# Strassen slots of a fused attention and MoE kernel: product 3 between 6 and 7, the two runs of 512-column products joined behind 7, product 4 last

## The chip, the core and the metric

The kernel runs on one core of a Trainium2 chip. The metric is device time in microseconds (us); three runs of the kernel before gave 1327.15, 1327.16 and 1327.39, the median is 1327.16. Engines are named as the profile names them: PE (TensorE matmuls), PEld (TensorE weight loads), DVE (VectorE), ACT (ScalarE), POOL (GpSimd), SP (SyncE, which issues the DMAs).

## What is computed

Three layers follow each other: a retention attention (2 batches, 8 heads, 768 positions), a mixture of 8 experts whose gate is normalised by 8 rounds of row and column scaling, and a feed-forward block with a tanh.

```python
x = attn_out.transpose(0, 2, 1, 3).reshape(1536, 512)
P = sinkhorn(exp(x @ w_gate - max))            # 1536 x 8
out = 0
for e in range(8):
    h = maximum(x @ w1[e], 0)                  # 1536x512 @ 512x1024
    out += P[:, e:e+1] * (h @ w2[e])           # 1536x1024 @ 1024x512
h = out @ w_in                                 # 1536x512 @ 512x2048
return (h - tanh(h)) @ w_out
```

The change lies in the expert loop.

## The kernel before

Operands are split into a high and a low part (`w1h`, `w1l`, `hhi`, `hlo`, ...), so that every product of two tiles is three matmuls: high by high, high by low, low by high.

**Slots.** The expert layer is a loop over 96 slots (`for s in range(NS)`, L585): 16 half experts `u`, 3 blocks `b` of 512 tokens, and `p` in (0, 1). One slot computes two 128x512 tiles of `h` from a 2 by 2 block product in Strassen's form with seven products. `product(ps, s, i, start)` (L572) issues product `i`: six matmuls of 256 columns (L579, L581, L582, twice) into a half of a PSUM bank. A slot has two banks, `pa` (named `ha` in the trace) and `pb` (`hb`), from a pool of four.

**What ties the products together inside a slot.** Product 1 goes to `pa` low; ACT copies it to `s12` low (L600). Products 2 and 5 go to the two halves of `pb`; ACT copies product 5 to `s5` (L607). Product 6 is added to `pa` low; ACT copies the sum to `s12` high (L609). Product 3 is added to `pb` high, over product 5, so it may start only when the copy to `s5` has read it. Product 7 is added to `pa` low, so it may start only when the copy to `s12` high has read that half. DVE then forms `pa` high from `pa` low and `s5` (L617), product 4 is added to `pa` low, and DVE adds `s12` to all of `pb` (L628). `pa` and `pb` are then the two rows of `h` before the ReLU. `relu_hi` (ACT, L508) and `relu_lo` (DVE, L513) write the high and low part of the ReLU to `hhi` and `hlo`, which have two buffers each.

**Second products.** A finished row is put on the list `parts`; `second` (L468) issues its twelve matmuls of 512 columns against `w2h` and `w2l` (L477, L478, L480) into four banks `yp`. After the second row of a slot with `p = 1` the four banks hold a finished sum and `evac` (L483, DVE) adds them to `yacc`, one call for each bank.

**Order of a slot before.** The order is written out by hand, and each engine runs its instructions in it: products 1, 2, 5, 6; the second products of the slot before's row `a` (12 matmuls); the helpers of `fill[s]`; product 7; the second products of the slot before's row `b` (12 matmuls); two calls of `evac`; the helpers of `fillb[s]`; product 4; product 3; two calls of `evac`; the helpers of `fillc[s]`. The row `b` of a slot gets its ReLU only in the next slot (`pend`). Only slot 0, which has no row behind it, runs products 1, 2, 5, 6, 3, 7, 4.

**Helpers.** `fill`, `fillb` and `fillc` hold, for each slot, the work of other stages: loading, summing and splitting the next expert's weights (`w_load`, `w_sum`, `w1_split`, `w2_split`), conversion of the last layer's weights (`conv`), the gate (`gate1`, `gate2`, `stage`, some with a small matmul), and in the first slots the splitting of the remaining tokens (`blocks1`, `blocks2`).

Of the kernel before, what the change touches and what calls it, by code (L numbers as in the profile page):

```python
# [14 lines left out]
ALU = mybir.AluOpType  # L15
# [12 lines left out]
TPB = BT // 128  # L28
# [22 lines left out]
def kernel(  # L51
# [9 lines left out]
    nc = tc.nc  # L61
# [10 lines left out]
    def bank(name):  # L72
        return psh.tile([128, 512], F32, tag="h", name=name)
# [107 lines left out]
    for i in range(12):  # L181
# [9 lines left out]
        out=g[:, 129:257], data0=lamt.to_broadcast([H, 128]), data1=one8, initial=1.0,  # L191
# [7 lines left out]
        out=dtab,  # L199
# [4 lines left out]
    for hh in range(2):  # L204
        src = gscr[:, 129:257].rearrange("(n two) m -> two n m", two=2)[hh]
        nc.sync.dma_start(
            out=lq[64 * hh:64 * hh + 64],
# [257 lines left out]
    parts = []  # L465


    def second(ps, tiles=range(TPB), late=False):  # L468
        for u, b, q, i, a, c, first, last in ps:
            if first and 0 in tiles:  # L470
                ypsum[u, b] = [psy.tile([128, 512], F32, tag=f"y{n}", name=f"yp{u}_{b}_{n}") for n in range(TPB)]
            for terms in ((0, 1), (2,)) if late else ((0, 1, 2),):
                for t in tiles:
                    ts = slice(128 * t, 128 * t + 128)
                    yp = ypsum[u, b][t]
                    if 0 in terms:
                        nc.tensor.matmul(out=yp, lhsT=a[:, ts], rhs=w2h[q][:, i], start=first, stop=False)  # L477
                        nc.tensor.matmul(out=yp, lhsT=a[:, ts], rhs=w2l[q][:, i], start=False, stop=False)  # L478
                    if 2 in terms:
                        nc.tensor.matmul(out=yp, lhsT=c[:, ts], rhs=w2h[q][:, i], start=False, stop=last)  # L480
        return (u, b) if last else None

    def evac(u, b, t):  # L483
        yp = ypsum[u, b]
        if t == 0 and u in (0, NU):
            yacc[b] = yp_.tile([128, TPB, DM], F32, tag=f"y{b}", name=f"yacc{u}_{b}")
        y = yacc[b][:, t]
        if u == 0:
            nc.vector.tensor_copy(out=y, in_=yp[t])
        elif u == NU:  # L490
            nc.scalar.activation(out=y, in_=yp[t], func=ACTF.Copy)
        elif u == 1 or u > NU:
            nc.vector.tensor_tensor(out=y, in0=yp[t], in1=y, op=ALU.add)
        else:
            nc.vector.scalar_tensor_tensor(out=y, in0=yp[t], scalar=prob[:, b * TPB + t, u // 2:u // 2 + 1], in1=y,  # L495
                                           op0=ALU.mult, op1=ALU.add)
        if u == NU + NQ - 1:
            n0 = t % B * S + (b * TPB + t) // B * CH
            nc.sync.dma_start(out=out[n0:n0 + 128, :], in_=y)
# [6 lines left out]
    def relu_hi(ps, name):  # L506
        a = hp.tile([128, 512], F32R, tag="hhi", name=f"hhi{name}")
        nc.scalar.activation(out=a, in_=ps, func=ACTF.Relu)  # L508
        return a

    def relu_lo(ps, a, name):
        c = hp.tile([128, 512], F32R, tag="hlo", name=f"hlo{name}")
        nc.vector.scalar_tensor_tensor(out=c, in0=ps, scalar=0.0, in1=a.bitcast(F32), op0=ALU.max, op1=ALU.subtract)  # L513
        return c
# [13 lines left out]
    fill = {s: [] for s in range(LASTS + 4)}  # L528
    fillb = {s: [] for s in range(LASTS + 4)}
# [34 lines left out]
    for n in range(nconv):  # L564
        s = s0 + n * (s1_ - s0) // nconv
# [6 lines left out]
    def product(ps, s, i, start):  # L572
        u, b, p = s // 6, s // 2 % 3, s % 2
        q = 2 * u + p
        kind, xi = XI[i]
        xh, xl = (x1[b][kind, j][:, xi].rearrange("p (k m) -> p k m", k=2) for j in range(2))
        for k in range(2):
            ws = slice(WI[i] + 128 * k, WI[i] + 128 * k + 128)
            nc.tensor.matmul(out=ps, lhsT=w1h[q][:, ws], rhs=xh[:, k], start=start and k == 0, stop=False,  # L579
                             skip_group_check=True)  # L580
            nc.tensor.matmul(out=ps, lhsT=w1h[q][:, ws], rhs=xl[:, k], start=False, stop=False, skip_group_check=True)  # L581
            nc.tensor.matmul(out=ps, lhsT=w1l[q][:, ws], rhs=xh[:, k], start=False, stop=k == 1, skip_group_check=True)  # L582

    pend = None
    for s in range(NS):  # L585
        if s == 1:
            yp_, sm = (ctx.enter_context(tc.tile_pool(name=n, bufs=1, reuse_waits="tile")) for n in ("yp", "sm"))
        if s == 4:
            attn.close()
            wps.append(ctx.enter_context(tc.tile_pool(name="wpc", bufs=1, reuse_waits="tile")))  # L590
            attn = ctx.enter_context(ExitStack())
            cp = attn.enter_context(tc.tile_pool(name="cp", bufs=1, side="right", reuse_waits="tile"))
        u, b, p = s // 6, s // 2 % 3, s % 2
        q = 2 * u + p
        pa, pb = bank(f"ha{s}"), bank(f"hb{s}")
        s12 = sn_.tile([128, 512], F32, tag="s12", name=f"s12_{s}")
        s5 = sn_.tile([128, 256], F32, tag="s5", name=f"s5_{s}")
        lo, hi = slice(0, 256), slice(256, 512)
        product(pa[:, lo], s, 1, True)
        nc.scalar.activation(out=s12[:, lo], in_=pa[:, lo], func=ACTF.Copy)  # L600
        if pend:
            hb = relu_hi(pend[0], f"b{s - 1}")
            lb = relu_lo(pend[0], hb, f"b{s - 1}")
            parts.append(pend[1] + (hb, lb, False, (s - 1) % 2 == 1))
        product(pb[:, lo], s, 2, True)
        product(pb[:, hi], s, 5, True)
        nc.scalar.activation(out=s5, in_=pb[:, hi], func=ACTF.Copy)  # L607
        product(pa[:, lo], s, 6, False)
        nc.scalar.activation(out=s12[:, hi], in_=pa[:, lo], func=ACTF.Copy)  # L609
        if pend:  # L610
            second([parts.pop(0)])
        for f in fill[s]:
            f()
        if s == 0:
            product(pb[:, hi], s, 3, False)
        product(pa[:, lo], s, 7, False)
        nc.vector.tensor_tensor(out=pa[:, hi], in0=pa[:, lo], in1=s5, op=ALU.add)  # L617
        done = second([parts.pop(0)]) if pend else None
        if done:
            evac(*done, 0)  # L620
            evac(*done, 1)
        for f in fillb[s]:
            f()
        product(pa[:, lo], s, 4, False)
        ha = relu_hi(pa, f"a{s}")
        if s > 0:
            product(pb[:, hi], s, 3, False)
        nc.vector.tensor_tensor(out=pb, in0=pb, in1=s12, op=ALU.add)  # L628
        la = relu_lo(pa, ha, f"a{s}")
        parts.append((u, b, q, 1, ha, la, p == 0, False))  # L630
        pend = (pb, (u, b, q, 0))
        if done:
            evac(*done, 2)
            evac(*done, 3)
        for f in fillc[s]:
            f()
    hb = relu_hi(pend[0], "bz")
    parts.append(pend[1] + (hb, relu_lo(pend[0], hb, "bz"), False, True))


    attn.close()
# [5 lines left out]
    def sub(v):  # L647
        u, b, f = NU + v // 12, v // 4 % 3, v % 4
        return u, b, 2 * u + f // 2, f % 2, f
# [32 lines left out]
    for v in range(NV + 2):  # L682
        if v < NV:
            u, b, q, i, f = sub(v)
# [10 lines left out]
        for part_ in due:  # L695
            done = second([part_], late=v == NV + 1)
# [52 lines left out]
```

## Time and profile before

| | |
|---|---|
| median of three runs | 1327.16 us |
| span of the profiled execution, first to last instruction | 1325.3 us |
| around the span (median less span; no separate total time of the profiled execution is given) | 1.9 us |
| PE busy | 1313.7 us, 99% of the span |
| DVE, ACT, POOL busy | 69%, 40%, 21% |
| TensorE clock granted | 0.998 of full speed in the mean |

The profile is one execution. Times of a row are counted from the span's first instruction. In the timeline a matmul's printed duration overlaps its successor's, since matmuls are pipelined; the distance from one start to the next is what a matmul costs the stream.

### The profile page before, as it was taken

To read this page: it belongs to the slowest core of one execution; us is meant where nothing else is said; L and a number is where in the kernel's file an instruction comes from. 1 tells how busy PE (TensorE), PEld (TensorE's weight loads), DVE (VectorE), ACT (ScalarE), POOL (GpSimd) and SP (SyncE) were. 2 spreads that over 40 slices of the span, in tenths; PEclk is the share of its full clock that TensorE was granted. 3 is DMA by queue.
4 is the path that set the end of the run, shared out by engine and by line. 5 is a ranking of instruction groups with operands and counts; after the bars stand their busy time and mean duration, and the time that the engine had idled before them with its cause. 6 is when DMAs were issued, how large, how long until landed. Compare 5 with 4: busy or idle time off the path is not lost.

```text
span 1325.3 us, 20925 instructions
## 1 busy us (share of the span) xinstructions
PE 1313.7 (99%) x8383; PEld 1163.0 (88%) x8383; DVE 913.2 (69%) x1698; ACT 527.9 (40%) x1029; POOL 274.1 (21%) x323
## 2 busy tenths in 40 slices
PE   8999999999999999999999999999999999999998
PEld 6889999999999999999999999999999888888887
DVE  4886676757657575757666675757654487788887
ACT  1443332233323232323322332323232578776764
POOL 4611011212213131222212221322210102020200
PEclk9999999999999999999999999999999999999999
DMA  9501120212312122212222132221211100000001
GB/s 299 173 32 33 33 72 25 69 59 65 100 55 81 57 68 61 76 56 69 72 64 68 57 100 69 69 68 57 69 36 33 33 32 32 32 32 32 32 32 64
DMA packets 37138, 85.00 MB, mean 64 GB/s; under 512 B 4136, under 2 KB 13872, under 8 KB 37040
## 3 DMA queue, kind: packets, MB, share of 16 engines
q1 hardware_dynamic: 37040, 83.67, 19.7%
q8 instruction: 65, 1.06, 0.3%
q14 instruction: 33, 0.27, 0.1%
HBM read 72.11 MB, written 11.55 MB: 63 GB/s over the span
## 4 chain that ended last, share of the span: by engine, by line
PE 96%; DVE 2%; DMA 1%; issue 0%; SPq 0%; ACT 0%; DVEq 0%; ACTq 0%
PE yp L480 16%; PE yp L477 16%; PE yp L478 16%; PE ha L579 7%; PE ha L582 7%; PE ha L581 7%; PE hb L579 5%; PE hb L581 5%; PE hb L582 5%; PE g L691 3%; PE g L689 3%; PE g L690 3%; DMA qkv<-in_qkv 1%; PE tr L523 0%; PE o L277 0%
## 5 line engine op out<-in xcount | busy, mean ns | idle before, releaser
L508 ACT ACTIVATE hhia<-ha 128x512 fp32r<-128x512 f32 x96 | 57.5, 599 | 469.9 <-PE ha L582 467.6
L579 PE MATMUL ha<-xsh,w1h 128*128 128x256 f32 x576 | 162.4, 282 | 1.7 <-ACT s L600 1.7
L582 PE MATMUL ha<-xsh,w1l 128*128 128x256 f32 x576 | 161.2, 280 | 0.0
L581 PE MATMUL ha<-xsl,w1h 128*128 128x256 f32 x576 | 160.8, 279 | 0.0
L456 POOL TENSOR_TENSOR c<-c,d 128x256 f32<-128x256 f32 x64 | 47.8, 746 | 544.0 <-DVE d L455 544.0
L478 PE MATMUL yp<-w2l,hhia 128*128 128x512 f32 x384 | 149.5, 389 | 0.0
L480 PE MATMUL yp<-w2h,hloa 128*128 128x512 f32 x384 | 149.5, 389 | 0.0
L477 PE MATMUL yp<-w2h,hhia 128*128 128x512 f32 x384 | 149.4, 389 | 0.0
L480 PE MATMUL yp<-w2h,hlob 128*128 128x512 f32 x380 | 148.7, 391 | 0.0
L478 PE MATMUL yp<-w2l,hhib 128*128 128x512 f32 x380 | 148.0, 390 | 0.0
L477 PE MATMUL yp<-w2h,hhib 128*128 128x512 f32 x380 | 147.9, 389 | 0.0
L617 DVE TENSOR_TENSOR ha<-ha,s 128x256 f32<-128x256 f32 x96 | 41.4, 432 | 141.2 <-PE ha L582 140.7
L628 DVE TENSOR_TENSOR hb<-hb,s 128x512 f32<-128x512 f32 x96 | 67.0, 697 | 91.5 <-PE hb L582 91.5
L495 DVE SCALAR_TENSOR_TENSOR yacc<-yp,prob,yacc 128x512 f32<-128x512 f32 x168 | 118.8, 747 | 9.0 <-PE yp L480 9.0
L579 PEld LDWEIGHTS ha<-xsh,w1h 128*128 128x128 f32 x576 | 108.2, 188 | 9.2 <-ACT s L600 1.9
L581 PEld LDWEIGHTS ha<-xsl,w1h 128*128 128x128 f32 x576 | 108.3, 188 | 7.4
L582 PEld LDWEIGHTS ha<-xsh,w1l 128*128 128x128 f32 x576 | 108.9, 189 | 0.0
L579 PE MATMUL hb<-xph,w1h 128*128 128x256 f32 x384 | 106.8, 278 | 0.0
L581 PE MATMUL hb<-xpl,w1h 128*128 128x256 f32 x384 | 106.4, 277 | 0.0
L582 PE MATMUL hb<-xph,w1l 128*128 128x256 f32 x384 | 106.2, 277 | 0.0
L480 PEld LDWEIGHTS yp<-w2h,hloa 128*128 128x128 f32 x384 | 72.1, 188 | 15.0
L480 PEld LDWEIGHTS yp<-w2h,hlob 128*128 128x128 f32 x380 | 71.4, 188 | 14.9
(159 smaller groups left out, 3332.8 us busy)
## 6 DMA issues: line engine op xcount, KB each, us to landing
wraw<-in_w SPq DMA_DIRECT2D x64, 512.0 KB, 4.7
d<-in_wio SPq DMA_DIRECT2D x64, 256.0 KB, 2.8
qkv<-in_qkv SPq DMA_DIRECT2D x23, 512.0 KB, 7.2
wscr<-c SPq DMA_DIRECT2D x64, 128.0 KB, 1.8
wraw<-wscr SPq DMA_DIRECT2D x16, 512.0 KB, 4.4
out<-yacc SPq DMA_DIRECT2D x12, 256.0 KB, 2.1
qkv<-in_qkv SPq DMA_DIRECT2D x2, 256.0 KB, 3.2
dtab<-gscr SPq DMA_DIRECT2D x1, 512.0 KB, 6.4
```

The lines of the kernel that those rows point to most:

```text
L456: nc.gpsimd.tensor_tensor(out=c1.bitcast(F32), in0=c1.bitcast(F32), in1=lo.bitcast(F32), op=ALU.mult)
L477: nc.tensor.matmul(out=yp, lhsT=a[:, ts], rhs=w2h[q][:, i], start=first, stop=False)
L478: nc.tensor.matmul(out=yp, lhsT=a[:, ts], rhs=w2l[q][:, i], start=False, stop=False)
L480: nc.tensor.matmul(out=yp, lhsT=c[:, ts], rhs=w2h[q][:, i], start=False, stop=last)
L495: nc.vector.scalar_tensor_tensor(out=y, in0=yp[t], scalar=prob[:, b * TPB + t, u // 2:u // 2 + 1], in1=y, op0=ALU.mult, op1=ALU.add)
L508: nc.scalar.activation(out=a, in_=ps, func=ACTF.Relu)
L579: nc.tensor.matmul(out=ps, lhsT=w1h[q][:, ws], rhs=xh[:, k], start=start and k == 0, stop=False, skip_group_check=True)
L581: nc.tensor.matmul(out=ps, lhsT=w1h[q][:, ws], rhs=xl[:, k], start=False, stop=False, skip_group_check=True)
L582: nc.tensor.matmul(out=ps, lhsT=w1l[q][:, ws], rhs=xh[:, k], start=False, stop=k == 1, skip_group_check=True)
L617: nc.vector.tensor_tensor(out=pa[:, hi], in0=pa[:, lo], in1=s5, op=ALU.add)
L628: nc.vector.tensor_tensor(out=pb, in0=pb, in1=s12, op=ALU.add)
L689: nc.tensor.matmul(out=ph, lhsT=w1h[q][:, ws], rhs=x2[b][0][:, k], start=k == 0, stop=False)
```

## The change

Slots 1 to 95 get the order 1, 2, 5, 6, 3, 7, then both rows of second products as one run of 24 matmuls, row `b` first, then the helpers of `fill[s]` and `fillb[s]`, then the ReLU of this slot's own row `b`, the four calls of `evac` where a sum is finished, product 4, the ReLU of row `a`, and the helpers of `fillc[s]`. `pend` is gone: row `b` is put on the list in its own slot. The flags for the first and the last part of a sum change places, because row `b` now comes first. The DVE sum into `pb` comes right behind product 3.

```diff
-        if pend:
-            hb = relu_hi(pend[0], f"b{s - 1}")
-            lb = relu_lo(pend[0], hb, f"b{s - 1}")
-            parts.append(pend[1] + (hb, lb, False, (s - 1) % 2 == 1))
         product(pb[:, lo], s, 2, True)
         product(pb[:, hi], s, 5, True)
         nc.scalar.activation(out=s5, in_=pb[:, hi], func=ACTF.Copy)
         product(pa[:, lo], s, 6, False)
         nc.scalar.activation(out=s12[:, hi], in_=pa[:, lo], func=ACTF.Copy)
-        if pend:
-            second([parts.pop(0)])
-        for f in fill[s]:
-            f()
-        if s == 0:
-            product(pb[:, hi], s, 3, False)
+        product(pb[:, hi], s, 3, False)
+        nc.vector.tensor_tensor(out=pb, in0=pb, in1=s12, op=ALU.add)
         product(pa[:, lo], s, 7, False)
         nc.vector.tensor_tensor(out=pa[:, hi], in0=pa[:, lo], in1=s5, op=ALU.add)
-        done = second([parts.pop(0)]) if pend else None
+        done = None
+        while parts:
+            done = second([parts.pop(0)])
+        for f in fill[s] + fillb[s]:
+            f()
+        hb = relu_hi(pb, f"b{s}")
+        parts.append((u, b, q, 0, hb, relu_lo(pb, hb, f"b{s}"), p == 0, False))
         if done:
-            evac(*done, 0)
-            evac(*done, 1)
-        for f in fillb[s]:
-            f()
+            for t in range(TPB):
+                evac(*done, t)
         product(pa[:, lo], s, 4, False)
         ha = relu_hi(pa, f"a{s}")
-        if s > 0:
-            product(pb[:, hi], s, 3, False)
-        nc.vector.tensor_tensor(out=pb, in0=pb, in1=s12, op=ALU.add)
-        la = relu_lo(pa, ha, f"a{s}")
-        parts.append((u, b, q, 1, ha, la, p == 0, False))
-        pend = (pb, (u, b, q, 0))
-        if done:
-            evac(*done, 2)
-            evac(*done, 3)
+        parts.append((u, b, q, 1, ha, relu_lo(pa, ha, f"a{s}"), False, p == 1))
         for f in fillc[s]:
             f()
-    hb = relu_hi(pend[0], "bz")
-    parts.append(pend[1] + (hb, relu_lo(pend[0], hb, "bz"), False, True))
```

## Rows read from the trace of the kernel before

**Rows 1.** The page: span, PE's busy time, the chain's share by engine.

```profile
span 1325.3 us, 20925 instructions
...
PE 1313.7 (99%) x8383; PEld 1163.0 (88%) x8383; DVE 913.2 (69%) x1698; ACT 527.9 (40%) x1029; POOL 274.1 (21%) x323
...
PE 96%; DVE 2%; DMA 1%; issue 0%; SPq 0%; ACT 0%; DVEq 0%; ACTq 0%
```

**Rows 2.** Busy time by stretch: slots 0 to 3, and slots 20 to 59.

```profile
60.57:100.53 39.96, 38.23 (x280) 34.47 (x278) 30.18 (x57) 19.62 (x40) 4.58 (x6) 1.00 0.08 27
...
266.98:678.07 411.09, 411.09 (x2643) 373.45 (x2641) 277.12 (x546) 129.38 (x269) 93.63 (x122) 1.00 0.22 69
```

**Rows 3.** Timeline of PE, one slot's turn: start, duration, line, tile.

```profile
604.52 0.40 PE L480 MATMUL yp<-w2h,hlob 128*128 128x512 f32 x1
604.76 0.28 PE L579 MATMUL ha<-xsh,w1h 128*128 128x256 f32 x1
...
605.46 0.28 PE L579 MATMUL hb<-xph,w1h 128*128 128x256 f32 x1
...
606.15 0.28 PE L579 MATMUL ha<-xph,w1h 128*128 128x256 f32 x1
...
608.08 0.28 PE L582 MATMUL hb<-xsh,w1l 128*128 128x256 f32 x1
...
608.88 0.39 PE L477 MATMUL yp<-w2h,hhia 128*128 128x512 f32 x1
...
611.60 0.28 PE L579 MATMUL ha<-xsh,w1h 128*128 128x256 f32 x1
...
612.30 0.39 PE L477 MATMUL yp<-w2h,hhib 128*128 128x512 f32 x1
```

**Rows 4.** Timeline of ACT in that slot: the copy to s5.

```profile
608.39 0.38 ACT L607 ACTIVATE s<-hb 128x256 f32<-128x256 f32 x1 [0.33 <-PE hb L582]
```

**Rows 5.** Timeline of PE, PEld and ACT in slot 0, products 6, 3, 7.

```profile
62.67 0.28 PE L582 MATMUL hb<-xsh,w1l 128*128 128x256 f32 x1
...
62.99 0.39 ACT L607 ACTIVATE s<-hb 128x256 f32<-128x256 f32 x1 [1.03 <-PE hb L582]
...
63.38 0.28 PE L582 MATMUL ha<-xsh,w1l 128*128 128x256 f32 x1
63.43 0.19 PEld L579 LDWEIGHTS hb<-xph,w1h 128*128 128x128 f32 x1
63.50 0.32 PE L579 MATMUL hb<-xph,w1h 128*128 128x256 f32 x1
...
63.65 0.28 PE L581 MATMUL hb<-xpl,w1h 128*128 128x256 f32 x1
...
64.11 0.28 PE L582 MATMUL hb<-xph,w1l 128*128 128x256 f32 x1
64.13 0.19 PEld L579 LDWEIGHTS ha<-xsh,w1h 128*128 128x128 f32 x1
...
64.36 0.28 PE L581 MATMUL ha<-xsl,w1h 128*128 128x256 f32 x1
...
64.83 0.28 PE L582 MATMUL ha<-xsh,w1l 128*128 128x256 f32 x1
```

**Rows 6.** Timeline of PE: product 1 of slot 1, right behind product 4.

```profile
66.96 0.28 PE L581 MATMUL ha<-xpl,w1h 128*128 128x256 f32 x1
...
67.53 0.28 PE L579 MATMUL hb<-xph,w1h 128*128 128x256 f32 x1
```

**Rows 7.** Timeline of DVE and PE, slots 3 and 4: tokens' low part and its reader.

```profile
97.57 1.22 DVE L133 TENSOR_TENSOR xsl<-ts,xsh 128x1024 fp32r<-128x1024 f32 x1
...
102.00 0.28 PE L581 MATMUL hb<-xsl,w1h 128*128 128x256 f32 x1
```

**Rows 8.** The page's groups: two of DVE's, busy, mean ns, idle before.

```profile
L628 DVE TENSOR_TENSOR hb<-hb,s 128x512 f32<-128x512 f32 x96 | 67.0, 697 | 91.5 <-PE hb L582 91.5
L495 DVE SCALAR_TENSOR_TENSOR yacc<-yp,prob,yacc 128x512 f32<-128x512 f32 x168 | 118.8, 747 | 9.0 <-PE yp L480 9.0
```

More of the change, by code (lines that the diff above doesn't have):

```diff
@@ L582, in product @@
             nc.tensor.matmul(out=ps, lhsT=w1l[q][:, ws], rhs=xh[:, k], start=False, stop=k == 1, skip_group_check=True)
-    pend = None
+    lo, hi = slice(0, 256), slice(256, 512)
     for s in range(NS):
@@ L597 @@
         s5 = sn_.tile([128, 256], F32, tag="s5", name=f"s5_{s}")
-        lo, hi = slice(0, 256), slice(256, 512)
         product(pa[:, lo], s, 1, True)
         nc.scalar.activation(out=s12[:, lo], in_=pa[:, lo], func=ACTF.Copy)
-        if pend:
-            hb = relu_hi(pend[0], f"b{s - 1}")
-            lb = relu_lo(pend[0], hb, f"b{s - 1}")
-            parts.append(pend[1] + (hb, lb, False, (s - 1) % 2 == 1))
         product(pb[:, lo], s, 2, True)
```

## The prediction

> **What bounds the kernel now.** I read the page first, then the busy times by stretch, then the timeline of PE at single matmuls, and last the timeline of slot 0, which already runs the order that the other slots are to get. PE is busy 1313.7 of 1325.3 us, and the chain that ended last is 96% PE [rows 1]. From slot 20 to slot 60 (the window is cut at the first matmul of product 1 in both) PE is busy for all of the 411.09 us [rows 2]: no wait opens a gap there, and a slot costs 411.09 / 40 = 10.277 us. So the time can change in two ways only: the pace of the stream, or a new wait in it.
>
> The pace is not the same everywhere, and this is what the reader is to see in the timeline. From 606.15 to 608.88 products 1, 2, 5 and 6 run in 2.73 us for 24 matmuls, 0.1135 each or 0.68 a product; a run of 512-column products takes 2.72 for 12, 0.227 each. Product 7, between the two runs, takes 0.70 (611.60 to 612.30), product 4, behind the second run, also 0.70 (604.76 to 605.46), and product 3 after it 0.69; the last matmul before product 4 takes 0.24 instead of 0.227 [rows 3]. So 256-column matmuls have a fast pace, 0.1133, and a slow one, about 0.1177, which they fall into behind a run of 512-column products. In these slots the slow pace ends as product 4 ends. Six slow matmuls cost 6 x 0.0044 = 0.026. The excess of a slot over the fast pace, 10.277 - 42 x 0.1133 - 24 x 0.2267 = 0.08, is then: product 7 0.026, product 4 0.026, the entry to product 4 0.01, the step back to fast in product 3 0.012, and 0.004 for each of the two passages from 256 to 512 columns (the matmul before a run takes about 0.117).
>
> **Part by part. The runs joined.** The number of matmuls is unchanged: 42 and 24 a slot. One of two passages into a 512-column run goes: -0.004 a slot. Product 7 no longer stands behind such a run, so its 0.026 could go too; whether it does hangs on the wait below. Product 4 still stands behind a run and keeps its slow pace; the twelve more matmuls ahead of it change nothing that a row shows. Behind it comes product 1 of the next slot instead of product 3. That passage occurs once in the trace, from slot 0 to slot 1, and there five matmuls of product 1 take 0.57 us, 0.114 each [rows 6]: the slow pace ends there too. Bounds: it ends as in that row (nothing), or it lasts to product 5 (18 x 0.0044 less 0.012, +0.067 a slot). I take the row.
>
> **Product 3 behind product 6.** Product 3 writes over what ACT copies to s5. Before, 42 matmuls lay between; now there is only product 6. PE runs in order, so a wait of product 3 holds all of the stream behind it. The length of that chain is in slot 0, which has the order 5, 6, 3, 7: the last matmul of product 5 starts at 62.67, ACT copies from 62.99 for 0.39, and the weight load of product 3 starts at 63.43, 0.05 after the copy: 0.76 in all. That load is late: loads otherwise start with the matmul ahead of them, here at 63.38; and the first matmul of product 3 takes 0.15 instead of 0.118 [rows 5]. In a later slot the copy begins 0.31 after product 5's last matmul (608.08) and lasts 0.38 [rows 3, 4]; with the same 0.05 the load can go 0.74 after that matmul. Product 6 at the fast pace covers 0.68. So 0.06 of stall in every slot, and 0.006 for the matmul behind it, which in slot 0 is slow too (four matmuls in 0.46, 63.65 to 64.11). Slot 0 bears the sum out: product 6 at the slow pace covers 0.71, the load is 0.05 late, and 0.03 is added. Bounds: 0 (the load is not held) and 0.066. I take 0.065.
>
> The trace shows the wait on the load itself: it starts 0.05 late, and the stall is visible [rows 5]. [...]
>
> **Product 7 behind product 3.** It waits for the copy to s12 high. In slot 0 its load starts 0.75 after product 6's last matmul (63.38 to 64.13), 0.02 after the matmul ahead of it, and product 7 then runs at the slow pace (four matmuls in 0.47) [rows 5]. In the new slots product 3, with its stall, covers 0.68 + 0.065 = 0.745: wait and cover meet, so I count no second stall. But the pace of product 7 is open: 0.026 gained a slot if it runs fast, nothing if it runs slow. The only row with product 7 behind 3 shows it slow; I take that. In the same row product 3 is fast behind its stall; the other bound, slow there too, adds 0.022.
>
> **What moves and costs nothing, and its cover.** DVE's sum into `pb` now comes right behind product 3, 0.70 each [rows 8], and is due only for the ReLU after both runs, 5.4 us later. The ReLU of row `b` waits for a buffer of `hhi` that the first of the two runs frees, and its reader is a whole slot away. The four evictions, 0.75 each [rows 8], stand behind the helpers and that ReLU on DVE; they are due one by one at the next slot's runs, 42 matmuls or 4.8 us after the last of the runs. DVE is busy 277.12 of 411.09 us, 6.9 a slot; four evictions are 3.0 and fall in every second slot, so such a slot has 1.5 more than the mean, some 8.4 of 10.28 [rows 2, 8], so the cover holds, with a margin of about 2 us. If it were gone, each 0.1 us by which evictions are late would cost 48 x 0.1 = 4.8 us. The helpers keep their order among themselves, so SP issues the same DMAs in the same order and POOL's queue is unchanged; the loads of weights that stand in `fillb` are issued earlier in the slot, since they wait for splits which now come sooner. ACT is busy 129.38 / 40 = 3.2 us a slot [rows 2] and free when product 5 ends.
>
> **Once, at the start.** In slot 3 the low part of the last tokens is written by DVE at 97.57 for 1.22 us, behind the gate's exponentials, whose small matmul stands in `fill`; it ends at 98.79, and slot 4's product 5 reads it from 102.00: 3.2 us of margin [rows 7]. That small matmul moves behind product 3 (0.69), product 7 (0.70) and the other run (2.73) [rows 3], 4.1 later, while the reader stays where it is: some +0.9 us of stall. The first four slots already hold 39.96 - 38.23 = 1.7 us of PE's gaps [rows 2], which I leave as they are: ACT's queue there is the same but for one ReLU. Bounds 0 and 2 us.
>
> **Sum.** 95 slots x (0.065 - 0.004) = 5.8; with the start 6.7. The profiled span of 1325.3 becomes 1332.0; with the 1.9 us that the median of the runs lies above that span, 1333.9, say 1334.0. Against 1327.16 that is +0.5%; the measurement tells about 0.2%, 2.7 us, from no change.
>
> **Rivals.**
> No stall (other side). The load goes ahead of the wait, or the copy ends before product 6 does; it decides if the gate falls by 0.06, to 0.68. Then nothing disturbs products 3 and 7, and 7 is fast: 95 x (-0.004 - 0.026) = -2.9, +0.9 at the start: 1325.2, no change that can be told. For it: only 0.06 is missing. Against: slot 0.
> Stall, but product 7 fast: wait and cover meet within 0.01, so the disturbance that made it slow in slot 0 may be missing: 95 x 0.026 = 2.5 less, 1331.5.
> Stall, with 3 and 7 slow: 95 x 0.022 = 2.1 more, 1336.1. For it: matmuls behind a stop are mostly slow (slot 0's product 7).
> The slow pace outlives product 4: 95 x 0.067 = 6.4 more, 1340.4. For it: in slot 0 product 6, three products after the start, was still slow (0.71 [rows 5]). Against: rows 6.
> The change does what it says and product 4 loses its slow pace as well: 95 x (0.026 + 0.01 + 0.012) = 4.6 less, 1329.4, within what can be told. For it nothing but that the cause of the slow pace isn't in the rows.
>
> **Chances.** My forecast, with 3 slow or not: 0.40. Product 7 fast: 0.20. Slow pace outlives product 4: 0.15. Product 4 fast: 0.10. No stall: 0.10; a gain beyond this, by gaps of the first slots that close: 0.05. The range of 1328 to 1341 leaves out the last two and some of the far ends of others, about 2 in 10. Faster 0.05; same 0.19 (no stall, and product 4 fast for the most part); slower 0.76.
>
> **What would show it.** Product 3's first weight load some 0.06 after the matmul ahead of it, and an entry "PE hb L579 <- ACT s" of the waits with about 95 times; product 6 at 0.68; product 1 behind 4 at 0.114 to 0.115; a slot of 10.34 us between slots 20 and 60; a new gap of about 1 us at slot 4. I am wrong if the load isn't late, if a slot is 10.25 us or less, if products 1, 2 and 5 run at 0.118, or if PE shows gaps at the head of the second products, which would be DVE's.

## The result, and the profile after

The changed kernel takes 1343.72 us (median of four runs, 1342.6 to 1344.35) against 1327.28 for the kernel before on the same chip: ratio 1.0121, 95% interval 1.0107 to 1.0134. It is slower by 1.2%, as forecast in sign, but by 16.4 us where 6.8 were forecast, and 1343.7 lies above the range.

The page of the changed kernel: span, PE's busy time, the chain's share by engine, as in [rows 1].

```profile
span 1342.3 us, 21130 instructions
...
PE 1326.3 (99%) x8383; PEld 1171.7 (87%) x8383; DVE 894.3 (67%) x1698; ACT 533.9 (40%) x1029; POOL 265.4 (20%) x323
...
PE 96%; DVE 2%; DMA 1%; issue 1%; ACT 0%; SPq 0%; DVEq 0%
```

The page alone says nothing of the loss: PE is busy 99% before and after. Busy time by stretch, cut at the first matmul of product 1 as in [rows 2]: slots 0 to 3, and slots 20 to 59. (The columns are the stretch and its length, the busy time and the number of instructions of PE, PEld, DVE, ACT and POOL, the granted clock, the share of the DMA engines and GB/s.)

```profile
61.73:101.77 40.04, 38.47 (x279) 34.61 (x278) 26.45 (x54) 18.31 (x39) 4.06 (x6) 1.00 0.08 27
272.21:687.94 415.73, 415.73 (x2642) 376.55 (x2641) 268.66 (x546) 132.34 (x268) 90.49 (x124) 1.00 0.22 68
```

A slot costs 415.73 / 40 = 10.393 instead of 10.277, and PE still shows no gap in it: the wait read below, some 0.06, is shorter than the 0.28 printed for the matmul ahead of it and so hidden in the busy time. Only the starts show it. The timeline of PE, PEld and ACT in one of these slots, to be held against [rows 3, 4] (the copy to s5, L607 before, is L602 here):

```profile
624.64 0.40 PE L480 MATMUL yp<-w2h,hloa 128*128 128x512 f32 x1
...
624.88 0.28 PE L579 MATMUL ha<-xsh,w1h 128*128 128x256 f32 x1
...
625.58 0.28 PE L579 MATMUL ha<-xph,w1h 128*128 128x256 f32 x1
...
626.27 0.28 PE L579 MATMUL hb<-xph,w1h 128*128 128x256 f32 x1
...
627.52 0.28 PE L582 MATMUL hb<-xsh,w1l 128*128 128x256 f32 x1
...
627.63 0.28 PE L579 MATMUL ha<-xsh,w1h 128*128 128x256 f32 x1
...
627.83 0.38 ACT L602 ACTIVATE s<-hb 128x256 f32<-128x256 f32 x1 [0.91 <-PE hb L582]
...
628.20 0.28 PE L582 MATMUL ha<-xsh,w1l 128*128 128x256 f32 x1
628.27 0.19 PEld L579 LDWEIGHTS hb<-xph,w1h 128*128 128x128 f32 x1
...
628.32 0.34 PE L579 MATMUL hb<-xph,w1h 128*128 128x256 f32 x1
...
628.49 0.28 PE L581 MATMUL hb<-xpl,w1h 128*128 128x256 f32 x1
...
628.96 0.19 PEld L579 LDWEIGHTS ha<-xsh,w1h 128*128 128x128 f32 x1
...
629.08 0.28 PE L579 MATMUL ha<-xsh,w1h 128*128 128x256 f32 x1
...
629.79 0.40 PE L477 MATMUL yp<-w2h,hhib 128*128 128x512 f32 x1
...
630.03 0.39 PE L478 MATMUL yp<-w2l,hhib 128*128 128x512 f32 x1
...
631.41 0.39 PE L478 MATMUL yp<-w2l,hhib 128*128 128x512 f32 x1
```

Product 5's last matmul starts at 627.52, ACT's copy to s5 ends at 628.21, and product 3's first load goes at 628.27, 0.07 after the matmul ahead of it (628.20) instead of with it. That matmul holds the stream from 628.32 to 628.49 (0.17, and 0.34 is printed instead of 0.28). Product 3 takes 0.76 (628.32 to 629.08) and product 7 0.71 (629.08 to 629.79): both at the slow pace. The first seven matmuls of the run behind them take 1.62 (629.79 to 631.41) where seven of 0.2267 take 1.587. In the medians of slots 14 to 89, taken from the starts, the slot's extra 0.120 divides so: product 3 +0.071 (a stall of 0.062, that is 0.175 for the held matmul instead of 0.113, and the slow pace 0.022, less 0.012 because the step back from slow to fast now falls in product 1), product 1 +0.012, the run of 24 +0.040, product 6 -0.004, product 7 +0.001.

The rest stands outside the ordinary slots. PE and ACT, three places: slot 4's product 5; slot 7's product 5; the end of slot 95's runs.

```profile
103.14 0.28 PE L579 MATMUL hb<-xsh,w1h 128*128 128x256 f32 x1
103.89 0.38 PE L581 MATMUL hb<-xsl,w1h 128*128 128x256 f32 x1 [0.48 <-DVE xsl L133]
...
133.98 1.06 ACT L132 ACTIVATE w1h<-wsum 128x1024 fp32r<-128x1024 f32 x1 [2.77 <-POOL wsum L112]
...
135.96 0.28 PE L581 MATMUL hb<-xsl,w1h 128*128 128x256 f32 x1
137.33 0.39 PE L582 MATMUL hb<-xsh,w1l 128*128 128x256 f32 x1 [1.09 <-DVE w1l L133]
...
1064.24 1.03 PE L523 MATMUL tr<-ident,yacc 128*128 128x128 f32 x8
1066.25 0.93 PE L523 MATMUL tr<-ident,yacc 128*128 128x128 f32 x5 [0.98 <-DVE x2l L133]
```

At each of them PE waits for a DVE instruction of a helper. The sum over the profiled execution: 95 ordinary extras of 0.120 are 11.4; slot 4 has 0.7 more than that, slot 7 1.4, and slots 93 to 95, where the transposes for the last layer stand, 0.4, 0.5 and 1.7 (slot 95 taken to the first matmul of the last layer). The first product starts 1.2 later (61.73 instead of 60.57), ahead of all changed code; in the kernels below that start lies between 59.5 and 61.7, so it is no effect. Together 17.3; slots 0, 1 and 42 are 0.4 shorter in all, and 17.0 is what the span grew by.

Slot 7's wait begins two slots earlier. The staging tile of the weights is loaded again (L103) when the second split of `w2` has read it. DVE and POOL in the kernel before, the end of that split and the first step of the sum that needs the load:

```profile
119.40 0.68 DVE L133 TENSOR_TENSOR w2l<-wraw,w2h 128x512 fp32r<-128x512 f32 x1
...
124.23 0.73 POOL L109 TENSOR_TENSOR wsum<-wraw 128x256 f32<-128x256 f32 x1 [39.82 <-DVE hlob L513]
```

The same after:

```profile
125.40 0.69 DVE L133 TENSOR_TENSOR w2l<-wraw,w2h 128x512 fp32r<-128x512 f32 x1
...
130.38 0.73 POOL L109 TENSOR_TENSOR wsum<-wraw 128x256 f32<-128x256 f32 x1 [41.52 <-DMA wraw<-in_w]
```

SP issues the load at 120.15 before and at 126.15 after, or 9.1 and 13.0 after the start of slot 5, and POOL's sum starts 4.1 and 4.2 behind it. On DVE the split stands behind a step of the gate, and that step's small matmul (L415) now stands behind both runs: DVE's waits for it come to 25.3 us in 8, before to 9.3 in 7.

### The profile page after: what moved, and what is told of

Read it like the earlier page. It is cut to its first block, busy times and chain, and to the rows that moved or that the text cites. A ratio compares the mean times of both kernels' runs of the same rounds, so it can differ in the third digit from the quotient of the medians.

```text
span 1342.3 us, 21130 instructions
## 1 busy us (share of the span) xinstructions
PE 1326.3 (99%) x8383; PEld 1171.7 (87%) x8383; DVE 894.3 (67%) x1698; ACT 533.9 (40%) x1029; POOL 265.4 (20%) x323
## 4 chain that ended last, share of the span: by engine, by line
PE 96%; DVE 2%; DMA 1%; issue 1%; ACT 0%; SPq 0%; DVEq 0%
PE yp L477 16%; PE yp L480 16%; PE yp L478 16%; PE ha L579 7%; PE ha L581 7%; PE ha L582 6%; PE hb L579 5%; PE hb L582 5%; PE hb L581 5%; PE g L674 3%; PE g L676 3%; PE g L675 3%; DMA qkv<-in_qkv 1%; PE o L272 1%; PE o L277 0%
## 5 line engine op out<-in xcount | busy, mean ns | idle before, releaser
L477 PE MATMUL yp<-w2h,hhib 128*128 128x512 f32 x384 | 151.4, 394 | 0.0
L606 DVE TENSOR_TENSOR hb<-hb,s 128x512 f32<-128x512 f32 x96 | 67.1, 699 | 125.7 <-PE hb L582 123.9
L508 ACT ACTIVATE hhib<-hb 128x512 fp32r<-128x512 f32 x96 | 57.4, 598 | 234.2 <-PE yp L478 226.1
L513 DVE SCALAR_TENSOR_TENSOR hloa<-ha,hhia 128x512 fp32r<-128x512 f32 x96 | 66.2, 689 | 115.6 <-ACT hhia L508 115.2
L495 DVE SCALAR_TENSOR_TENSOR yacc<-yp,prob,yacc 128x512 f32<-128x512 f32 x168 | 114.1, 742 | 0.0
L579 PE MATMUL hb<-xph,w1h 128*128 128x256 f32 x384 | 112.2, 292 | 0.0
L513 DVE SCALAR_TENSOR_TENSOR hlob<-hb,hhib 128x512 fp32r<-128x512 f32 x96 | 66.0, 687 | 34.9 <-ACT hhib L508 34.5
```

## Experiments

Each runs beside the kernel before (medians 1326.9 to 1327.1). "The slot" is the mean of slots 20 to 59, from the starts on PE.

**Take the waits away.** e1 gives products 3 and 7 a bank of their own, so that no copy has to be done before them. What it leaves out of `h`: product 3 from row `b`, product 7 from the first half of row `a`, products 1 and 6 from its second half.

```diff
-        product(pb[:, hi], s, 3, False)
+        pc = bank(f"hc{s}")
+        product(pc[:, hi], s, 3, True)
...
-        product(pa[:, lo], s, 7, False)
-        nc.vector.tensor_tensor(out=pa[:, hi], in0=pa[:, lo], in1=s5, op=ALU.add)
+        product(pc[:, lo], s, 7, False)
+        nc.vector.tensor_tensor(out=pa[:, hi], in0=pc[:, lo], in1=s5, op=ALU.add)
```

> The changed kernel, but products 3 and 7 go to a third bank that no copy reads, so that neither waits for ACT; the sum with s5 reads product 7 from there. Left out: product 3 and product 6's share no longer reach the two rows of h; all matmuls, copies and DVE steps stay. Theory (the wait is the root of what a slot lost: product 3 held 0.06, then slow, product 7 slow, and the run's first seven matmuls 0.04 dearer because they follow the slow pace): product 3 falls from 0.763 to 0.68, product 7 from 0.709 to 0.684, the 24 matmuls from 5.486 to 5.45, a slot from 10.393 to 10.25, the total from 1343.7 to about 1330. Rival (the run's 0.04 comes from the exchanged buffers of hhi and hlo, product 7's pace from its operands): the run stays at 5.486, product 7 at 0.709, a slot at 10.31, total 1336.

1333.62, ratio 1.0049 [1.0032, 1.0066]; the slot 10.247. PE's timeline, the starts of products 3 and 7 and of the run:

```profile
633.64 0.28 PE L579 MATMUL hc<-xph,w1h 128*128 128x256 f32 x1
...
634.32 0.28 PE L579 MATMUL hc<-xsh,w1h 128*128 128x256 f32 x1
...
635.00 0.39 PE L477 MATMUL yp<-w2h,hhib 128*128 128x512 f32 x1
```

0.68 and 0.68: without the wait, 3 and 7 are fast, and the run's extra 0.04 is gone as well. So all three parts of the slot's loss hang on the wait. The total still lies above before for two reasons of 4 to 5 us each. The helpers stand where the changed kernel has them, and slots 4, 7 and 93 to 95 have its excess again (0.7 and 1.4 in slots 4 and 7). And with a third bank a slot, from a pool of four, slots 2, 5, 6, 8, 10 and 11 lose 0.3 to 0.9 each that the changed kernel does not lose; three times PE is seen to wait, at product 3, for the DVE half of a ReLU (L513), 1.5 us in all.

**Buffers, or product 3 alone.** With the rows exchanged, `hhib` and `hhia` lie in each other's buffers; e2 sets them back by taking one buffer of each ahead of the loop. e3 is the kernel before with product 3 moved behind 6 and nothing else.

```diff
+    for tag in ("hhi", "hlo"):
+        turned = hp.tile([128, 512], F32, tag=tag, name=f"turned{tag}")
+        nc.vector.memset(turned[:, 0:1], 0.0)
```

> The changed kernel with one unused tile ahead of the slots in hhi and in hlo, so that rows a and b take the buffers that they had in the kernel before. Theory (the wait is the root): nothing changes, run of 24 matmuls 5.486, slot 10.393, total 1343.7. Rival (the buffers' addresses make the run's first seven matmuls dearer): the run falls to 5.446, a slot to 10.353, total 1340.

> The kernel before with one part of the change: product 3 directly behind product 6 in every slot, with its DVE sum, the two runs kept apart. Theory (the wait is the root, joining the runs is nearly free): product 3 takes 0.763 instead of 0.692, product 1 behind product 4 takes 0.692 instead of 0.680, a slot 10.35 to 10.40, total 1334.5 to 1339. Rival (the loss comes from joining the runs and turning their order): product 3 costs at most 0.065 more and then regains it, total 1327 to 1331.

e2: 1343.65, ratio 1.0125 [1.0110, 1.0141], the same slot of 10.393: the buffers play no part. e3: 1337.60, ratio 1.0078 [1.0063, 1.0093], the slot 10.391, as good as with all of the change (the median of its slots is 10.393 in both). The extra 0.04 sits in whatever run stands behind the slow product 3, here row `a` (PE's timeline):

```profile
654.67 0.34 PE L579 MATMUL hb<-xph,w1h 128*128 128x256 f32 x1
...
655.43 0.40 PE L477 MATMUL yp<-w2h,hhia 128*128 128x512 f32 x1
...
657.06 0.39 PE L478 MATMUL yp<-w2l,hhia 128*128 128x512 f32 x1
```

Seven matmuls in 1.63. So joining the runs costs a slot nothing and gives it nothing; product 3's move is the whole loss of a slot.

**The helpers.** e4 puts `fill[s]` between the two rows of the run.

```diff
-        while parts:
+        if parts:
+            second([parts.pop(0)])
+        for f in fill[s]:
+            f()
+        if parts:
             done = second([parts.pop(0)])
-        for f in fill[s] + fillb[s]:
+        for f in fillb[s]:
             f()
```

> The changed kernel with the helpers of fill between the two runs instead of behind both. Theory (beside 0.12 in each of 95 slots, some 4.5 us are lost once: at slot 4 0.75, at slot 7 1.4, at the last slots 2.5, since helpers with a matmul come 2.7 us later): slots stay at 10.393, these gaps shrink, total 1339.5 to 1341.5. Rival (the gaps come from the later ReLU of row b or from ACT's queue): total 1343 to 1344.

1339.30 (four runs, 1337.0 to 1342.6), ratio 1.0094 [1.0076, 1.0112]; the slot 10.393, but slots 4 and 7 now 10.65 (11.36 and 12.04 in the changed kernel) and slots 93 and 94 11.31 and 11.29 (11.70 and 11.82). 4.4 us come back of the 4.8 that the three places had lost; 0.5 stays in slot 95. The runs scatter by more than that, so it is the slots of the trace that carry this reading: the helpers' place was the cause there.

**More cover, first try.** e5 issues product 4 one slot late, five matmuls behind the run and the sixth between 6 and 3; e6 puts all of it between 6 and 3. Both have `fill[s]` as in e4, and the ReLU of row `a` moves with product 4.

```diff
+        if late:
+            product(late[0][:, lo], s - 1, 4, False, range(5))   # e6: range(0)
         product(pa[:, lo], s, 1, True)
...
         product(pa[:, lo], s, 6, False)
         nc.scalar.activation(out=s12[:, hi], in_=pa[:, lo], func=ACTF.Copy)
+        if late:
+            product(late[0][:, lo], s - 1, 4, False, range(5, 6))   # e6: range(0, 6)
...
-        product(pa[:, lo], s, 4, False)
...
+        late = (pa, (u, b, q, 1))
```

> Product 4 of a slot is issued one slot later and cut in two: five of its six matmuls directly behind the 512-column run, its last matmul between products 6 and 3; fill[s] stands between the two rows of the run. Theory (the loss in each slot is the wait of product 3 for ScalarE's copy and the slow pace that the wait leaves behind): between product 5's end and product 3 there are now 0.680 of product 6 and 0.113 of one matmul, 0.793, more than the 0.74 that the copy chain took, so nothing waits: product 3 at 0.680, product 7 at 0.684 or less, the run at 5.45, a slot 10.25, in all about 1325 with before at 1327. Rival (the slow pace behind the run ends only with the whole of product 4): products 1, 2, 5 at 0.706, up to 0.08 more in a slot, about 1332.

> The whole of product 4, one slot late, between products 6 and 3; products 1, 2, 5 and 6 directly behind the run. Theory (behind a run the pace is slow until product 4 has run): 1, 2, 5, 6 at 0.706, no wait of product 3, a slot 10.35, about 1335 in all. Rival (the slow pace ends after some seven matmuls whatever their operands): product 1 slow, the others 0.680, a slot 10.25, about 1325.

e5: 1342.69, ratio 1.0119 [1.0104, 1.0134], the slot 10.433: neither forecast, though the rival had named the slow products behind the run. Product 3 did not wait (its first matmul took 0.118), but all 42 matmuls of 256 columns ran at 0.1175, and the run had its extra 0.04. e6: 1334.65, ratio 1.0057 [1.0040, 1.0074], the slot 10.347, by the theory: 1, 2, 5, 6 and 4 slow, no wait, and the pace fast again from product 3's fourth matmul on. So in e6 the pace behind the run lasted until a whole product 4 had run; in e5 five of its matmuls did not end it (0.1175 behind them).

**What ends the slow pace.** Product 4's weight columns lie eight columns out of line with the others (`4: 1536 + 8`). e7 removes that from the changed kernel. e11 takes e6, with `fill[s]` as there, and gives the eight columns to product 1, which is first behind the run there.

```diff
-WI = {1: 0, 2: 256, 3: 1280, 4: 1536 + 8, 5: 512, 6: 768, 7: 1024}
+WI = {1: 0, 2: 256, 3: 1280, 4: 1536, 5: 512, 6: 768, 7: 1024}       # e7
+WI = {1: 1536 + 8, 2: 0, 3: 1280, 4: 256, 5: 512, 6: 768, 7: 1024}   # e11
```

> The changed kernel with the weight columns of product 4 in line with those of the other products instead of shifted by eight columns. Theory (the shift has a part in ending the slow pace behind product 4): products 1, 2, 5, 6 at 0.706, the wait of product 3 only 0.035, products 3 and 7 near 0.74 and 0.68 to 0.71, the run without the extra 0.04, so about the same slot of 10.39 by another division, about 1343. Rival (the shift has no part): product 1 at 0.692, the others at 0.680, product 3 at 0.763, as in the changed kernel.

> The order of e6_4between (1, 2, 5, 6, the slot before's 4, 3, 7, run of 24 with fill[s] between its rows), but the eight columns of shift are given to product 1, the first behind the run, instead of product 4. Theory (the slow pace behind a run ends where a whole product with shifted weight columns gives way to one without): products 1 and the start of 2 slow, all others 0.680, no wait, the run at 5.45, a slot 10.25; with the 1 us that e6 lost outside the ordinary slots, about 1325 to 1326. Rival (it is product 4's own operands that end it, or its place behind the run): 1, 2, 5, 6 and 4 at 0.706 as in e6, a slot of 10.35 or more, about 1335.

e7: 1345.13 (two runs), ratio 1.0137 [1.0117, 1.0157], the slot 10.413. Products 1, 2, 5 and 6 stay at 0.707, where 2, 5 and 6 take 0.680 in the changed kernel: in these slots the columns do end the pace. Product 3 comes at the slow pace here, and its wait turns the pace the other way; product 7 then waits too (PE's timeline):

```profile
628.93 0.28 PE L582 MATMUL ha<-xsh,w1l 128*128 128x256 f32 x1
629.05 0.31 PE L579 MATMUL hb<-xph,w1h 128*128 128x256 f32 x1
629.20 0.28 PE L581 MATMUL hb<-xpl,w1h 128*128 128x256 f32 x1
...
629.54 0.28 PE L581 MATMUL hb<-xpl,w1h 128*128 128x256 f32 x1
629.66 0.28 PE L582 MATMUL hb<-xph,w1l 128*128 128x256 f32 x1
629.77 0.30 PE L579 MATMUL ha<-xsh,w1h 128*128 128x256 f32 x1
629.91 0.28 PE L581 MATMUL ha<-xsl,w1h 128*128 128x256 f32 x1
```

0.15 for product 3's held matmul, 0.113 to 0.114 behind it; 0.14 for product 7's, and behind it, in the medians, 0.120, 0.117, 0.116 and 0.114, back toward the fast pace. The run has no extra. e11: 1325.20 (11 runs) against 1327.14 (15 runs), ratio 0.9986 [0.9977, 0.9995], 1.9 us less and the only one that beats the kernel before. Its slots 20 to 59 by stretch (columns as in [rows 2]), and PE's timeline from product 1 behind the run to product 6:

```profile
266.74:676.61 409.87, 409.87 (x2642) 372.14 (x2640) 263.42 (x544) 132.19 (x268) 93.00 (x123) 1.00 0.23 69
```

```profile
635.39 0.40 PE L480 MATMUL yp<-w2h,hloa 128*128 128x512 f32 x1
635.62 0.28 PE L581 MATMUL ha<-xph,w1h 128*128 128x256 f32 x1
...
636.32 0.28 PE L581 MATMUL hb<-xph,w1h 128*128 128x256 f32 x1
...
637.02 0.28 PE L581 MATMUL hb<-xsh,w1h 128*128 128x256 f32 x1
...
637.70 0.28 PE L581 MATMUL ha<-xsh,w1h 128*128 128x256 f32 x1
```

10.247 a slot: product 1 0.703, product 2 0.692 with the step back, then 0.68 for each product up to 7 (medians). Against e6 only the table of weight columns and the order in which the weights are split into it differ, and 9.4 us: 94 x 0.100.

**More cover, second try.** Product 2 has no copy waiting for it, so its matmuls were to be the cover. e8 and e10 run 1, 5, four matmuls of 2, 6, 3, two of 2, 7; e9 only exchanges 2 and 5. All have `fill[s]` as in e4. In e8 and e9 the start flag of product 2 now follows product 5 in the same bank, and their output is no longer that of the kernel before (off by a relative 1.50 in both); in e10 product 2 has no flag.

```diff
-        product(pb[:, lo], s, 2, True)
         product(pb[:, hi], s, 5, True)
         nc.scalar.activation(out=s5, in_=pb[:, hi], func=ACTF.Copy)
+        product(pb[:, lo], s, 2, True, range(4))   # e9: all six; e10: False
...
         product(pb[:, hi], s, 3, False)
+        product(pb[:, lo], s, 2, True, range(4, 6))   # not in e9
```

> The changed kernel with the order 1, 5, four matmuls of 2, 6, 3, the last two matmuls of 2, 7 (product 2 has no copy waiting for it), and fill[s] between the rows of the run. Theory (the loss of a slot is the wait of 3, and the slow pace that it leaves): 3 now has ten matmuls or 1.13 us between product 5 and itself, 7 has eight or 0.91 between product 6 and itself, both more than the 0.75 of the copy; product 4 stays whole behind the run and ends the slow pace. No wait, 3 and 7 at 0.680, the run at 5.45, a slot 10.25, 0.03 less than before: about 1324 to 1325, before 1327. Rival (moving the products, not the wait, makes the slow pace): 3 and 7 at 0.706 and the run with its extra 0.04, a slot 10.33, about 1333.

> Only products 2 and 5 exchanged (1, 5, 2, 6, 3, 7), and fill[s] between the rows of the run. Product 3 now has 2 and 6 as cover, 1.36, and doesn't wait; product 7 has only 3 behind 6, 0.68 against 0.75. Theory (a wait of some 0.06 costs itself, and the slow pace behind it until the run's seventh matmul, wherever it stands): product 7 at 0.76, the run with its extra 0.04, product 3 at 0.680, a slot 10.37, about 1337. Rival (only the wait at product 3 does this): 7 at 0.745 at most, the run at 5.45, a slot 10.31, about 1331.

> As e8_split2, but product 2's first matmul carries no start flag (product 5's, ahead of it in the same bank, does), so that nothing has to read the bank before product 2 may begin. Order 1, 5, four matmuls of 2, 6, 3, two matmuls of 2, 7; fill[s] between the rows of the run. Theory: no wait in the slot, 3 and 7 at 0.680, the run at 5.45, a slot 10.25 against 10.27 to 10.28 before, in all about 1324 to 1325. Rival (one of the moved products waits after all, or the moves make the slow pace themselves): a slot of 10.33 or more, 1332 or more.

1399.52, 1411.57 and 1400.79: ratios 1.0549 [1.0534, 1.0563], 1.0640 [1.0626, 1.0655] and 1.0553 [1.0538, 1.0567]. None was forecast. Product 2, which writes the other half of the bank that ACT is copying from, waits for that copy, flag or no flag (PE's timeline of e10):

```profile
638.02 0.28 PE L581 MATMUL hb<-xsh,w1l 128*128 128x256 f32 x1
638.77 0.39 PE L581 MATMUL hb<-xph,w1h 128*128 128x256 f32 x1 [0.47 <-ACT s L601]
```

0.75 from start to start, of which PE stands idle for 0.47; 96 times, 47.4 us in all, in each of the three. What would happen without that wait no run shows. The part that was to be tested is still readable, since the three share that wait. In e8 and e10 products 3 and 7 do not wait, are fast, and the run has no extra: slot 11.015 in e10. In e9 product 7 waits, with product 3 alone as its cover:

```profile
634.14 0.34 PE L579 MATMUL ha<-xsh,w1h 128*128 128x256 f32 x1
634.32 0.28 PE L581 MATMUL ha<-xsl,w1h 128*128 128x256 f32 x1
...
634.91 0.40 PE L477 MATMUL yp<-w2h,hhib 128*128 128x512 f32 x1
635.15 0.39 PE L478 MATMUL yp<-w2l,hhib 128*128 128x512 f32 x1
```

Again 0.175 for the held matmul in the median, 0.118 behind it and 0.24 for the first of the run; the slot is 11.133, 0.118 above e10. So a wait of 0.06 behind matmuls at the fast pace cost about 0.12 a slot at product 7 (0.118) as at product 3 (0.120), and it is not product 3 that is special.

## Why the prediction was right in sign and wrong in size

Forecast and measurement lie 9.6 us apart. Three terms come to about that much: product 3's slow pace behind its stall (2.1, taken at nothing), the first matmuls of the run behind a slow product (3.8, not in the sum), and the helpers (4.8 where 0.9 stood in the sum, for slot 4).

**The stall: right.** Forecast 0.06, measured 0.062; the load is 0.07 late. The chain from product 5's last matmul to the load is 0.75, forecast 0.74, and product 6 covers 0.68. The rival without a stall falls: the load did not go ahead of the wait, it went at 628.27, 0.06 behind the end of the copy (628.21). No second stall at product 7, as forecast: its load starts with the matmul ahead, at 628.96.

**Product 3 fast behind its stall: wrong, and the step that fails first.** It was read off [rows 5], where product 3 is fast. But there the matmuls ahead of the stall were slow, and in the new slots they are fast. A short wait turned the pace over in both directions: from slow to fast in slot 0 (0.1175 ahead, 0.114 behind) and in e7, from fast to slow in the ordinary slots of the changed kernel (0.113 ahead, 0.1175 behind), in e3 and in e9. The row was of the right order and of the other state. The waits were not of one length either (the held matmul took 0.03 more than the slow pace in slot 0 and e7, 0.06 more than the fast one in the others), so which of the two decides is not shown. The text kept the other bound, 0.022; that is the one measured.

**The run behind products 3 and 7: a term that the sum did not have.** 0.040 a slot, 3.8 us in all. Nothing in the trace of before shows it, since behind the slow product 7 there the run is at 0.227 from its first matmul on. Of the rivals, "3 and 7 slow" (1336.1) named the right pace and had no price for the run.

The slot, then: forecast 0.065 - 0.004 = 0.061; measured 0.062 + 0.022 + 0.040 - 0.004 = 0.120; over 95 slots 11.4 instead of 5.8.

**"What moves and costs nothing": half wrong.** The evictions and the sums are hidden, as forecast. The page's groups of DVE after, as in [rows 8] (L606 is L628 before):

```profile
L606 DVE TENSOR_TENSOR hb<-hb,s 128x512 f32<-128x512 f32 x96 | 67.1, 699 | 125.7 <-PE hb L582 123.9
...
L495 DVE SCALAR_TENSOR_TENSOR yacc<-yp,prob,yacc 128x512 f32<-128x512 f32 x168 | 114.1, 742 | 0.0
```

The evictions start with no idle time before them, and no product or run waits for one in an ordinary slot. The helpers are not hidden. Slot 4 lost 0.7, where 0.9 was forecast by that very mechanism. The same mechanism, a helper that comes a run later while its reader stays, was not followed into slot 7 (1.4; the load, the sum and the split of weights) and into slots 93 to 95 (2.7; the transposes). The text kept the helpers' order and looked at the queues of SP and POOL, and did not ask each helper's reader how much time it had. Its sentence that the loads in `fillb` would be issued earlier in the slot is wrong where it mattered: in slot 5 the load went 3.9 later (13.0 instead of 9.1 after the slot's start), since the split that it waits for came later; POOL's sum then waited for the load, and PE in slot 7 for the split behind that sum.

**Slow pace behind product 4: right.** Product 1 there takes 0.692, or 0.115 a matmul, and 2, 5 and 6 take 0.680. The rival in which the pace outlives product 4 fell for these slots; e7 shows what it hung on. The rival in which product 4 loses its pace as well fell too (0.703). **What would show it:** the entry of the waits with 95 times did not appear; that view books only gaps in which PE has nothing running, and here none is left open (0.062 of wait under the 0.28 printed for the matmul ahead).

## What to carry to other kernels

Where a stream is busy 99%, read the starts and not the busy time: a wait of 0.06 stood in no busy time and in no entry of the waits, only in the distance between starts, and cost 0.12 a slot, twice its own length, through the pace that it left. Before a row is carried over to a new place, look at the state that it was taken in (what pace ran ahead of it), not only at its order. And for every helper that moves, take its reader's time: the moves cost 4.8 us here, of which 0.9 had been counted, and putting `fill` back between the rows gave 4.4.

## What the runs showed of the hardware

- 256-column matmuls showed two paces, 0.1133 and 0.1175 from start to start, at a granted clock of 1.00 in either (slots 20 to 59 of e11, where nearly all are fast, and of e5, where all are slow). Behind a run of 512-column matmuls they ran at the slow one (before, in the medians, product 7 took 0.709 and product 4 0.703). In the ordinary slots it ended behind a whole product whose weight columns lie eight columns out of line with the next one's (product 4, or product 1 in e11: 0.680 for the products from the second behind it on), and not behind five of its six matmuls (e5, 0.1175) or without the eight columns (e7, 0.707 a product). Nor did it end behind product 4 of slots 4 to 11 of the changed kernel, where the gate's small matmul (L415) stands between the run and product 4: products 1 and 2 behind it take 0.706 to 0.707.
- A short wait turned the pace over, either way: from slow to fast where it held a matmul for 0.03 (slot 0 before, e7; 0.114 behind it), from fast to slow where it held one for 0.06 (the changed kernel, e3, e9; 0.1175 to 0.118 behind it). It did not do so everywhere: in slots 5, 6 and 8 to 12 of the changed kernel a matmul held for 0.036 behind slow ones has 0.117 to 0.118 behind it, and in e3 the matmuls behind the one that is held at 633.94 take 0.114. A wait of some 0.03 behind fast matmuls, at product 7, left the slow pace in slot 0 before (0.1175) and only a passing one in e7 (0.120 falling to 0.114). After the longer wait in e10 (0.75 from start to start) the first matmul took 0.22, the next four 0.117 to 0.122, and then the pace was fast.
- A run of 512 columns behind matmuls at the slow pace took 0.04 more over its first seven matmuls in the changed kernel, e3, e5 and e9, but not behind the slow product 7 between the two runs of the kernel before and of e3. What tells these cases apart, and why the eight columns end the pace, stays open; no run here settles it.
